# Attention backward on one core: dK, the dS transposes and dQ of a cell one step later, with their K load and dK store, and a fourth dS buffer

## The chip, the cores and the metric

One core of one Trainium2 chip. The metric is the device time of one execution in microseconds (us). All executions of the full kernels that are used here were classed as fast (not over 1.5% above the fastest execution of the same kernel beside them). Ratios are always the mean time of one kernel's fast runs over the mean of the other's fast runs of the same rounds, so they are not quite the ratio of the medians that stand beside them.

## The reference

Two independent attention blocks, A and B, forward and backward; all data are bf16. Cut to what matters:

```python
# per block: B, Sq, D = 8, 96, 640;  H, Sk, Dh = 32, 512, 128
q = (x @ wq).reshape(B, Sq, H, Dh).transpose(0, 2, 1, 3)
scores = jnp.einsum("bhqd,bhkd->bhqk", q, k_cache) * (Dh ** -0.5)
p = softmax(scores)
o = jnp.einsum("bhqk,bhkd->bhqd", p, v_cache)
out = o.transpose(0, 2, 1, 3).reshape(B, Sq, H * Dh) @ wo
# result: out of both blocks side by side, and the gradients of
# x, k_cache, v_cache, wq, wo of both blocks (jax.vjp)
```

## The kernel before

A *cell* is one head and one batch entry: 2 blocks x 32 heads x 8 entries = 512 cells. The kernel is a software pipeline. Every part of a cell is put into a list under a *step* number, the list is sorted by step and by a slot within the step, and is then emitted. A new cell starts in every step. Transfers serve two heads at once, a *pair* of cells, so each kind of transfer is issued once in two steps: its offset in `OFF` being even or odd decides which of the two.

```python
OFF = dict(kt=-1, vt=2, vn=1, kn=4, dv=7, dk=10, s2=3, s3=3, s4=4, s5=5, s6=6, s7=7, s8=8)
...
if j == 0:                                   # first cell of a pair
    em.add(ct + OFF["kt"], SLOTS["LOAD"], p_ldT(h, b, 0))         # K by DMA transpose
    em.add(ct + OFF["vt"], SLOTS["LOAD"], p_ldT(h, b, 1))         # V by DMA transpose
    em.add(ct + OFF["vn"], SLOTS["LOAD"] + 0.1, p_ldn(h, b, 1))   # V plain
    em.add(ct + OFF["kn"], SLOTS["LOAD"] + 0.1, p_ldn(h, b, 0))   # K plain
    em.add(ct + OFF["dv"], SLOTS["LOAD"] + 0.2, p_st(h, b, 1))    # store dV
    em.add(ct + OFF["dk"], SLOTS["LOAD"] + 0.2, p_st(h, b, 0))    # store dK
```

All six go through one queue, that of the sync engine, in the order of emission: `pools["sp"]` chains every transfer to the one before it. The transposed loads, the stores and their buffers:

```python
# p_ldT: 16 rows x (f d) of HBM -> [128, 64, 16], 4 buffers each for KT and VT
t_ = kvp.tile([128, F4 * KC, 16], BF16, name=key + "_p", bufs=4)
sp(nc.sync.dma_start_transpose(t_[:], src))
# p_st: dK and dV of a pair, 256 KB
sp(nc.sync.dma_start(dst.rearrange("h (p c) d -> p h (c d)", c=KC), t_[:]))
if which == 0:                               # after the dK store the cell's record is dropped
    for j in range(HP):
        CS.pop((blk, h + j, b))
...
st["dK_p"] = wk.tile([128, HP, KC * 128], BF16, name="dK_sb", bufs=3)   # three pairs of dK
```

The end of a cell. `c_s6` (offset s6) makes dP on TensorE and dS on VectorE. `c_s78` holds dQ of the cell at s8 and the transposes of dS of the cell at s7. `c_s7` (s7) makes dK from dS:

```python
# c_s6
nc.tensor.matmul(dP_ps[:], hs["dOT_h"][:, tok], st["VT"], start=True, stop=True)          # L386
dS_sb = wk.tile([Sq, Sk], BF16, name="dS_sb", bufs=3)
nc.vector.scalar_tensor_tensor(dS_sb..., dP_ps..., dl_ps[:, 0:1], st["P_sb"]..., ...)      # L390
# c_s78
nc.tensor.matmul(dQT_ps, st["K_sb"][:, c, :], st["dST_sb"]..., ...)                        # L405, dQ at s8
nc.tensor.transpose(dST_ps..., dS_sb[:, c * 128:(c + 1) * 128], ident[0:Sq, 0:Sq])         # L412, at s7
# c_s7
nc.tensor.matmul(dK_ps..., dS_sb..., hs["Qnat_h"]..., start=True, stop=True)               # L428
nc.scalar.activation(dK_p[:, j], dK_ps[:], ACT.Identity, scale=1.0)                        # L433
```

Projections, weight gradients and the output products of each head ("head work") are spread over the steps between these.

Of the kernel before, what the change touches and what calls it, by code (L numbers as in the profile page):

```python
# [11 lines left out]
BF16 = mybir.dt.bfloat16  # L12
# [28 lines left out]
SL_GRP = 95  # L41
SL_SETUP = 96

OFF = dict(kt=-1, vt=2, vn=1, kn=4, dv=7, dk=10, s2=3, s3=3, s4=4, s5=5, s6=6, s7=7, s8=8)
HP = 2
HK = [
    dict(pA=-10, pB=-7, pC0=[-6, -4], pC1=[-5, -3], pD1=-2, pD0=0, qA0=21, qA1=25, qB=[28, 25]),
# [24 lines left out]
def build_block(tc, em, tick0, blk, x, kc, vc, wq, wo, g_all, out_all, dx, dk, dv, dwq, dwo, ident, ones, pools, HG=4, first=True, groups=None):  # L72
    nc = tc.nc
    B, Sq, D = x.shape
    _, H, Sk, Dh = kc.shape
# [34 lines left out]
    const, ps, kvp, wk, hd, hst, grp = (pools[k] for k in ("const", "ps", "kvp", "wk", "hd", "hst", "grp"))  # L110

    def bank(shape, dt, name):
        return ps.tile(shape, dt, name=name, tag="bank")
# [75 lines left out]
    def pB(h):  # L189
        def f():  # L190
            st = HS[(blk, h)]
            woT_ps = bank([128, DC * 128], BF16, "woT_ps")
            for c in range(DC):
                nc.tensor.transpose(woT_ps[:, c * 128:(c + 1) * 128], st["wo_h"][:, c * 128:(c + 1) * 128], ident[:])
            woT_h = hd.tile([128, DC * 128], BF16, name="woT_h", bufs=1)
            evac(EV["pB0"], woT_h[:], woT_ps[:])
            st["woT_h"] = woT_h
            wqT_ps = bank([128, DC * 128], BF16, "wqT_ps")
            for c in range(DC):
                nc.tensor.transpose(wqT_ps[:, c * 128:(c + 1) * 128], st["wq_h"][:, c, :], ident[:])  # L200
            wqT_h = hst.tile([128, D], BF16, name="wqT_h")
            evac(EV["pB1"], wqT_h[:], wqT_ps[:])
            st["wqT_h"] = wqT_h
            st["QT_h"] = hd.tile([128, T], BF16, name="QT_h", bufs=4)
            st["dOT_h"] = hd.tile([128, T], BF16, name="dOT_h", bufs=4)
        return f
# [39 lines left out]
    def p_ldT(h, b, which):  # L246
        def f():
            key = "KT" if which == 0 else "VT"
            t_ = kvp.tile([128, F4 * KC, 16], BF16, name=key + "_p", bufs=4)
            src = (kc if which == 0 else vc)[b, h:h + HP].rearrange("h (r f) d -> (h r) (f d)", r=R8)  # L250
            sp(nc.sync.dma_start_transpose(t_[:], src))
            for j in range(HP):
                half = t_[:, :, j * R8:(j + 1) * R8]
                CS.setdefault((blk, h + j, b), {})[key] = half.rearrange("p (f c) r -> p f c r", c=KC)
        return f

    def p_ldn(h, b, which):
        def f():
            key = "K_sb" if which == 0 else "V_sb"
            t_ = kvp.tile([128, HP, KC, 128], BF16, name=key, bufs=4)  # L260
            src = (kc if which == 0 else vc)[b, h:h + HP]
            sp(nc.sync.dma_start(t_[:].rearrange("p h c d -> p h (c d)"), src.rearrange("h (p c) d -> p h (c d)", c=KC)))
            for j in range(HP):
                CS[(blk, h + j, b)][key] = t_[:, j]
        return f

    def p_st(h, b, which):
        def f():
            t_ = CS[(blk, h, b)]["dV_p" if which == 1 else "dK_p"]
            dst = (dv if which == 1 else dk)[b, h:h + HP]  # L270
            sp(nc.sync.dma_start(dst.rearrange("h (p c) d -> p h (c d)", c=KC), t_[:]))
            if which == 0:
                for j in range(HP):
                    CS.pop((blk, h + j, b))
        return f

    def h_alloc(h):
        def f():
            st = HS[(blk, h)]
            st["OT_h"] = hst.tile([128, T], BF16, name="OT_h", bufs=6)  # L280
            st["dQT_h"] = hst.tile([128, T], BF16, name="dQT_h")
        return f
# [97 lines left out]
    def c_s6(h, b):  # L380
        def f():
            st = CS[(blk, h, b)]
            hs = HS[(blk, h)]
            tok = slice(b * Sq, (b + 1) * Sq)
            dP_ps = bank([Sq, Sk], F32, "dP_ps")
            nc.tensor.matmul(dP_ps[:], hs["dOT_h"][:, tok], st["VT"], start=True, stop=True)  # L386
            dl_ps = bank([Sq, 1], F32, "dl_ps")
            nc.tensor.matmul(dl_ps[:], st["prod"][:], ones[:, 0:1], start=True, stop=True)  # L388
            dS_sb = wk.tile([Sq, Sk], BF16, name="dS_sb", bufs=3)
            nc.vector.scalar_tensor_tensor(dS_sb[:].rearrange("q (a f) -> q a f", f=F4), dP_ps[:].rearrange("q (f a) -> q a f", f=F4), dl_ps[:, 0:1],  # L390
                                           st["P_sb"][:].rearrange("q (a f) -> q a f", f=F4), op0=ALU.subtract, op1=ALU.mult)
            st["dS_sb"] = dS_sb
        return f
# [139 lines left out]
    for g in range(NG):  # L533
        h0 = GH0[g]
        for hh in range(groups[g]):
# [5 lines left out]
            em.add(c0t + hk["pB"], SL_HEAD, pB(h))  # L541
            em.add(c0t + OFF["s5"], SL_LOAD, h_alloc(h))
            for si in range(NTS):
# [4 lines left out]
            for b in range(B):  # L548
                ct = c0t + b * HP + j
                if j == 0:  # L550
                    em.add(ct + OFF["kt"], SLOTS["LOAD"], p_ldT(h, b, 0))
                    em.add(ct + OFF["vt"], SLOTS["LOAD"], p_ldT(h, b, 1))
                    em.add(ct + OFF["vn"], SLOTS["LOAD"] + 0.1, p_ldn(h, b, 1))
                    em.add(ct + OFF["kn"], SLOTS["LOAD"] + 0.1, p_ldn(h, b, 0))
                    em.add(ct + OFF["dv"], SLOTS["LOAD"] + 0.2, p_st(h, b, 1))
                    em.add(ct + OFF["dk"], SLOTS["LOAD"] + 0.2, p_st(h, b, 0))
# [156 lines left out]
```

## Time and profile before

| | kernel before |
|---|---|
| median of its first 3 timed runs | 1679.27 us (1679.18 to 1683.99) |
| span of the profiled run, a fourth (1674.12 us) | 1672.3 us, granted clock 0.994 |
| TensorE (PE) / VectorE (DVE) / ScalarE (ACT) / GpSimd (POOL) busy | 96 / 82 / 80 / 32% |
| dS transposes (L412) starting late, summed | 31.1 us |
| sum of all transfer issues of the one queue | 1460 us of 1672 |

The last row is worked out from the instruction records of the trace. A matmul starts late by its distance from the matmul before it, less the columns of that one divided by 2.4 per ns; gaps over 20 ns are summed. (The rate comes out of this trace: the median distance is 42 ns behind a matmul of 96 columns and 216 ns behind one of 512, so 416 columns more take 174 ns.)

From the page of the kernel before: part 1, the line of the sync engine's queue in part 3 (packets, MB, and the time of its packets as a share of the span of the 16 DMA engines), the first line of part 4 (the chain that ended last), and two groups of part 5, whose columns are busy time and mean ns of one, then idle time before it and what ended most of it.

```profile
PE 1607.8 (96%) x20640; PEld 1265.2 (76%) x20860; DVE 1366.7 (82%) x3381; ACT 1336.2 (80%) x3511; POOL 533.8 (32%) x1030
...
q1 hardware_dynamic: 378112, 454.57, 102.3%
...
PE 88%; DVE 5%; DMA 2%; issue 2%; ACT 2%; POOL 0%; SPq 0%; ACTq 0%; DVEq 0%
...
L433 ACT ACTIVATE dK_sb<-dK_ps 128x512 bf16<-128x512 f32 x512 | 303.2, 592 | 154.6 <-PE dK_ps L428 140.9
...
L412 PE MATMUL dq_dst_ps<-ident,dS_sb 96*128 96x96 bf16 x2048 | 173.2, 207 | 20.5 <-DVE dS_sb L390 20.3
```

By this chain TensorE is what bounds the kernel, and when it idles in mid-run, it is mostly before L412, for dS. From the waits of the kernel before (who waited for whom; us in total, times, longest):

```profile
ACT dK_sb L433 <- PE dK_ps L428: 140.9, 132, 2.7
...
PEld L412 <- DVE dS_sb L390: 27.0, 45, 1.5
...
PE dq_dst_ps L412 <- DVE dS_sb L390: 20.3, 43, 1.3
...
ACT dK_sb L433 <- DMA out_dram<-dK_sb: 10.4, 3, 4.9
```

One of these stalls in the timeline of the kernel before (start, duration in us, engine, line; in brackets the idle time and what ended it): dQ is done, and the transposes wait until dS, which began at 382.54, is there.

```profile
382.48 0.33 PE L405 MATMUL dq_dst_ps<-dST_sb,K_sb 128*128 128x96 bf16 x4
...
382.54 0.73 DVE L390 SCALAR_TENSOR_TENSOR dS_sb<-dP_ps,dl_ps,P_sb 96x512 bf16<-96x512 f32 x1
...
383.33 0.34 PE L412 MATMUL dq_dst_ps<-ident,dS_sb 96*128 96x96 bf16 x4 [0.52 <-DVE dS_sb L390]
```

The one DMA queue (SPq) of the kernel before in the timeline. These durations are the issue alone. The Trainium skill, "Perfetto Trace Analysis", section "Summary: the profiler window per engine type", says that the reported window of such a transfer hides the data movement, and the trace agrees: these issues take 0.4 to 1.7 us, while the median from issue to landing of a KT transpose is 5.1 us.

```profile
390.03 0.42 SPq L271 DMA_DIRECT2D out_dram<-dK_sb  x1
390.54 1.71 SPq L251 DMA_TRANSPOSE KT_p<-in_A_k_cache_dram  x1
392.35 0.53 SPq L262 DMA_DIRECT2D V_sb<-in_A_v_cache_dram  x1
392.97 0.42 SPq L271 DMA_DIRECT2D out_dram<-dV_sb  x1
393.48 1.17 SPq L251 DMA_TRANSPOSE VT_p<-in_A_v_cache_dram  x1
394.70 1.18 SPq L262 DMA_DIRECT2D K_sb<-in_A_k_cache_dram  x1
```

The two transposes of a pair, KT and VT, stand apart, with a load and a store between them on both sides.

### The profile page before, as it was taken

How to read it: one execution, taken by the hardware profiler on the slowest of the kernel's cores; microseconds unless marked ns; L12 is line 12 of the kernel's file. 1: busy time of each engine (PE TensorE's matmuls, PEld its weight loads, DVE VectorE, ACT ScalarE, POOL GpSimd, SP SyncE). 2: the span in 40 equal slices, each digit the busy share in tenths (PEclk: the TensorE clock that was granted, in tenths of full speed). 3: DMA queues.
4: the chain of work that ended last, by engine and by line, in shares of the span. 5: the costliest groups of instructions: out<-in, count | busy, mean ns of one | idle time of the engine just before them, and what ended most of it. 6: DMA issues, size and time to landing. Idle time of an engine off the chain costs nothing.

```text
span 1672.3 us, 55383 instructions
## 1 busy us (share of the span) xinstructions
PE 1607.8 (96%) x20640; PEld 1265.2 (76%) x20860; DVE 1366.7 (82%) x3381; ACT 1336.2 (80%) x3511; POOL 533.8 (32%) x1030
## 2 busy tenths in 40 slices
PE   6999999999999999999898999999999999999998
PEld 5777777777777787777676878777777777777776
DVE  4886888888888888888687778888888888888886
ACT  6988877879788787877776889788787877879783
POOL 2432333333233233333222333233333333333231
PEclk9999999999999999999899999999999999999999
DMA  9999999999999999999999999999999999999994
GB/s 247 283 266 285 266 268 296 297 270 275 271 279 281 285 268 292 265 284 233 275 290 297 295 266 272 278 287 274 274 291 281 278 286 281 283 274 273 282 271 139
DMA packets 378383, 458.13 MB, mean 274 GB/s; under 512 B 44288, under 2 KB 369920, under 8 KB 369920
## 3 DMA queue, kind: packets, MB, share of 16 engines
q1 hardware_dynamic: 378112, 454.57, 102.3%
q8 instruction: 163, 2.67, 0.7%
q14 instruction: 108, 0.88, 0.2%
HBM read 159.12 MB, written 159.12 MB: 190 GB/s over the span
## 4 chain that ended last, share of the span: by engine, by line
PE 88%; DVE 5%; DMA 2%; issue 2%; ACT 2%; POOL 0%; SPq 0%; ACTq 0%; DVEq 0%
PE q_ps L224 12%; PE o_ps L511 11%; PE dK_ps L428 6%; PE dV_ps L362 6%; PE dP_ps L386 6%; PE S_ps L291 6%; PE dwo_ps L466 6%; PE dwq_ps L486 6%; PE dq_dst_ps L412 5%; PE optp_ps L345 5%; PE optp_ps L338 5%; PE dq_dst_ps L405 4%; PE n_ps L239 4%; PE nat_ps L452 3%; DVE dS_sb L390 2%
## 5 line engine op out<-in xcount | busy, mean ns | idle before, releaser
L322 POOL TENSOR_SCALAR P_sb<-E_sb,rinv 96x512 bf16<-96x512 bf16 x512 | 352.5, 688 | 322.8 <-DVE rinv L313 321.6
L303 ACT ACTIVATE E_sb<-S_ps,negm 96x512 bf16<-96x512 f32 x512 | 348.2, 680 | 112.8 <-DVE negm L293 107.7
L376 POOL TENSOR_TENSOR prod<-OT_h,dOT_h 128x96 bf16<-128x96 bf16 x512 | 186.7, 365 | 784.6 <-DVE OT_h L348 768.1
L433 ACT ACTIVATE dK_sb<-dK_ps 128x512 bf16<-128x512 f32 x512 | 303.2, 592 | 154.6 <-PE dK_ps L428 140.9
L390 DVE SCALAR_TENSOR_TENSOR dS_sb<-dP_ps,dl_ps,P_sb 96x512 bf16<-96x512 f32 x512 | 383.2, 748 | 29.0 <-PE dl_ps L388 18.6
L293 DVE TENSOR_REDUCE negm<-S_ps 96x1 f32<-96x512 f32 x512 | 347.3, 678 | 60.7 <-PE S_ps L291 60.4
L367 ACT ACTIVATE dV_sb<-dV_ps 128x512 bf16<-128x512 f32 x512 | 308.1, 602 | 1.5 <-DMA out_dram<-dV_sb 1.3
L351 ACT ACTIVATE PT_sb<-optp_ps 128x384 bf16<-128x384 bf16 x512 | 251.7, 492 | 0.6 <-PE optp_ps L345 0.5
L414 DVE COPY dST_sb<-dq_dst_ps 128x384 bf16<-128x384 bf16 x512 | 177.6, 347 | 31.3 <-PE dq_dst_ps L412 28.8
L291 PE MATMUL S_ps<-KT_p,QT_h 128*96 128x512 bf16 x512 | 194.7, 380 | 5.7 <-ACT dK_sb L433 5.2
L428 PE MATMUL dK_ps<-Qnat_h,dS_sb 96*128 96x128 bf16 x2048 | 198.6, 220 | 0.4 <-ACT dK_sb L433 0.4
L362 PE MATMUL dV_ps<-dOnat_h,P_sb 96*128 96x128 bf16 x2048 | 198.7, 219 | 0.0
L386 PE MATMUL dP_ps<-VT_p,dOT_h 128*96 128x512 bf16 x512 | 195.7, 382 | 0.0
L412 PE MATMUL dq_dst_ps<-ident,dS_sb 96*128 96x96 bf16 x2048 | 173.2, 207 | 20.5 <-DVE dS_sb L390 20.3
L405 PEld LDWEIGHTS <-K_sb 128*128 128x128 bf16 x2048 | 133.9, 98 | 55.7 <-issue 9.5
L345 PE MATMUL optp_ps<-ident,P_sb 96*128 96x96 bf16 x2048 | 172.1, 205 | 2.2 <-POOL P_sb L322 1.5
L338 PE MATMUL optp_ps<-PT_sb,V_sb 128*128 128x96 bf16 x2048 | 172.6, 206 | 0.9 <-ACT PT_sb L351 0.8
L405 PE MATMUL dq_dst_ps<-dST_sb,K_sb 128*128 128x96 bf16 x2048 | 171.3, 206 | 0.0
L348 DVE CAST OT_h<-optp_ps 128x96 bf16<-128x96 f32 x512 | 127.0, 248 | 32.5 <-PE optp_ps L345 26.3
L511 PE MATMUL o_ps<-wo_r,OT_h 128*128 128x128 bf16 (+1 forms) x722 | 144.9, 295 | 2.5
L511 PE MATMUL o_ps<-wqT_h,dQT_h 128*128 128x128 bf16 (+1 forms) x721 | 144.4, 294 | 2.5
L224 PE MATMUL q_ps<-gT,woT_h 128*128 128x256 bf16 (+1 forms) x609 | 134.4, 324 | 9.7 <-DMA gT<-in_grad_out_dram 8.0
(66 smaller groups left out, 3012.8 us busy)
## 6 DMA issues: line engine op xcount, KB each, us to landing
out_dram<-dV_sb SPq DMA_DIRECT2D x256, 256.0 KB, 4.5
out_dram<-dK_sb SPq DMA_DIRECT2D x256, 256.0 KB, 4.5
V_sb<-in_A_v_cache_dram SPq DMA_DIRECT2D x128, 256.0 KB, 4.3
K_sb<-in_A_k_cache_dram SPq DMA_DIRECT2D x128, 256.0 KB, 4.4
V_sb<-in_B_v_cache_dram SPq DMA_DIRECT2D x128, 256.0 KB, 4.3
K_sb<-in_B_k_cache_dram SPq DMA_DIRECT2D x128, 256.0 KB, 4.3
out_dram<-dwo_sb SPq DMA_DIRECT2D x64, 160.0 KB, 4.6
out_dram<-dwq_sb SPq DMA_DIRECT2D x32, 320.0 KB, 4.5
```

Source lines behind the costliest of these rows:

```text
L224: nc.tensor.matmul(q_ps[:], lhs(c), rhsT[:, c, t0:t0 + w], start=(c == 0), stop=(c == DC - 1))
L293: nc.vector.tensor_reduce(negm[:], S_ps[:], axis=AX.X, op=ALU.max, negate=True)
L303: nc.scalar.activation(E_sb[:].rearrange("q (a f) -> q a f", f=F4), st["S_ps"][:].rearrange("q (f a) -> q a f", f=F4), ACT.Exp, bias=st["n ...
L322: nc.gpsimd.tensor_scalar(P_sb[:], st["E_sb"][:], st["rinv"][:], 0.0, op0=ALU.mult, op1=ALU.add)
L362: nc.tensor.matmul(dV_ps[:, c * 128:(c + 1) * 128], P_sb[:, c * 128:(c + 1) * 128], hs["dOnat_h"][:, b * 128:(b + 1) * 128], start=True, s ...
L367: nc.scalar.activation(dV_p[:, j], dV_ps[:], ACT.Identity, scale=1.0)
L386: nc.tensor.matmul(dP_ps[:], hs["dOT_h"][:, tok], st["VT"], start=True, stop=True)
L390: nc.vector.scalar_tensor_tensor(dS_sb[:].rearrange("q (a f) -> q a f", f=F4), dP_ps[:].rearrange("q (f a) -> q a f", f=F4), dl_ps[:, 0:1] ...
L405: nc.tensor.matmul(dQT_ps, st["K_sb"][:, c, :], st["dST_sb"][:, c * Sq:(c + 1) * Sq], start=(c == 0), stop=(c == KC - 1))
L428: nc.tensor.matmul(dK_ps[:, c * 128:(c + 1) * 128], dS_sb[:, c * 128:(c + 1) * 128], hs["Qnat_h"][:, b * 128:(b + 1) * 128], start=True, s ...
L433: nc.scalar.activation(dK_p[:, j], dK_ps[:], ACT.Identity, scale=1.0)
L511: nc.tensor.matmul(o_ps[:], src[:, t * 128:(t + 1) * 128], rhs, start=(hh == 0), stop=(hh == groups[g] - 1))
```

## The change

The intent: the dS transposes should not wait for a dS that was only just made. dK, the dS transposes and dQ of a cell move one step later (s7, s8), dS lives one step longer and gets a fourth buffer. The K load, which feeds dQ, and the dK store follow by one step; the dK store has to, because it drops the cell's record.

```diff
-OFF = dict(kt=-1, vt=2, vn=1, kn=4, dv=7, dk=10, s2=3, s3=3, s4=4, s5=5, s6=6, s7=7, s8=8)
+OFF = dict(kt=-1, vt=2, vn=1, kn=5, dv=7, dk=11, s2=3, s3=3, s4=4, s5=5, s6=6, s7=8, s8=9)
...
-            dS_sb = wk.tile([Sq, Sk], BF16, name="dS_sb", bufs=3)
+            dS_sb = wk.tile([Sq, Sk], BF16, name="dS_sb", bufs=4)
```

## The prediction

> **What bounds the kernel now.** TensorE. The page shows PE busy 96% of 1672.3 us, DVE 82%, ACT 80%, POOL 32%; the chain of waits is 88% PE, 5% DVE, 2% each DMA, ACT and issue. Busy share overstates PE (the Trainium skill, "Perfetto Trace Analysis", section "Identifying the Most-Contended Engine"), so I used start-to-start times. In full stretches four 96-column matmuls take 0.17 us, 43 ns each, which agrees with columns / 2.4 GHz + about 2.5 ns ("TensorE: Matmul & The Clock Gate", "Wait — 56ns, not 53.3ns?"). Over the whole trace the streamed columns come to 1465 us and the small per-matmul excess to 56 us; the remaining 139 us are gaps before matmuls that started over 20 ns late. Those before the dS transposes (line 412) are 31.1 us: 7.3 in the first 130 us, 7.6 from 130 to 785, 2.7 to 1000, 8.2 to 1615, 5.2 in the tail. The list of waits agrees: PE weight loads of line 412 waited 27.0 us for DVE dS (45 times), the matmuls 20.3 (43 times). In the steady state it recurs twice per four heads (100.8 us): a visible 0.52 us where a cell step has no head work, and 0.25 us.
>
> **What the change does.** It adds and removes no work. A step's PE order stays dQ, dS transposes, dK, O, P transposes, dV, dP, S, but the dS it uses was made two steps ago (a step is 2.2 to 4.5 us) instead of just before, behind dP (0.38), the wait for the row sum and DVE's 0.75 us. So that wait should vanish. The fourth dS buffer keeps DVE from waiting for dK. K load and dK store move with their users, so distances in steps (4 from load to use, 2 from dK to store) stay; the transfers bunch in odd steps, but the in-order queue runs ahead of them anyway. The dx groups follow one step later as well: the last of them (4 matmuls, about 0.33 us) then falls in the very step that had no head work and showed the 0.52 us stall.
>
> **How much is on the critical path.** At most about 31 us. Not all returns: in those light steps ACT's own work is near the step's length (in the tail 0.33 us idle of 2.59 us), and its P^T copy or POOL's P becomes the next thing PE waits for. Estimate by region: tail about 8 steps x 0.3 = 2.5 us; start 4 of 7; steady 11 of 18. Sum 17 us; minus 1 to 2 us for one more step at the drain. Hiccups around 120, 797 and 915 us (ACT waiting for dK_sb's store, 10.4 us in 3 waits; the second block's gT) stay, give or take 4 us.
>
> **Predicted:** 1665 us, 8 times in 10 between 1655 and 1677. Faster by over 2%: 0.04; within 2%: 0.94; slower by over 2%: 0.02.
>
> **Signs that each step is right.** PE's wait of line 412 for dS falls from 20.3 us to under 3, the weight loads' from 27.0 to under 4. ACT's wait for dK_ps (140.9 us, 132 times) falls by 10 to 30. New PE waits at lines 338 (ACT PT_sb) and 345 (POOL P_sb), 3 to 10 us together. Tail steps shorten from 2.58 to about 2.3 us. Busy times per engine and ns per instruction unchanged within 1%. Nothing of the DMA becomes a large new wait.
>
> **What would make it wrong.** If light steps are bound by ACT or DVE throughput, the wait only changes its name and the gain is under 5 us. If bunched transfers make dK_sb's or K's landing later, ACT or line 405 waits for a DMA and the change may be lost. If many small late starts elsewhere (line 224 32.6 us, 511 21.5 us) are echoes of dS, the gain exceeds 25 us.

## More of the kernel before

The two lines of the instructions on tile KT_p, kernel before (one per block; shortest, median and longest issue in ns):

```profile
L251 SPq DMA_TRANSPOSE KT_p<-in_A_k_cache_dram x128: 1102/1197/3641, 4.3 to 807.4; - x128
L251 SPq DMA_TRANSPOSE KT_p<-in_B_k_cache_dram x128: 1106/1187/2971, 814.0 to 1619.3; - x128
```

## The result, and the profile after

The changed kernel took 1739.99 us (median of 4 runs, 1735.23 to 1752.61) beside 1681.63 us for the kernel before: ratio 1.0354, 95% interval 1.0288 to 1.0419. It is slower by 3.5%, and outside the predicted range.

From the page of the changed kernel, the same lines:

```profile
PE 1626.3 (94%) x20670; PEld 1274.0 (73%) x20860; DVE 1367.1 (79%) x3381; ACT 1333.8 (77%) x3511; POOL 533.4 (31%) x1030
...
PE 67%; DMA 12%; ACT 9%; DVE 6%; issue 5%; SPq 0%; POOL 0%; ACTq 0%; DVEq 0%; POOLq 0%
...
L433 ACT ACTIVATE dK_sb<-dK_ps 128x512 bf16<-128x512 f32 x512 | 304.7, 595 | 248.8 <-PE dK_ps L428 152.8
...
L412 PE MATMUL dq_dst_ps<-ident,dS_sb 96*128 96x96 bf16 x2048 | 173.7, 207 | 0.0
```

The idle time before L412 has gone from 20.5 us to 0.0, as intended; its late starts fell from 31.1 to 1.4 us. But DMA now has 12% of the chain where it had 2%. The waits of the changed kernel:

```profile
ACT dK_sb L433 <- PE dK_ps L428: 152.8, 121, 2.7
ACT dK_sb L433 <- DMA out_dram<-dK_sb: 91.3, 53, 6.3
...
PE dwo_ps L466 <- ACT dK_sb L433: 29.8, 15, 3.1
...
PE woT_ps L194 <- ACT dK_sb L433: 14.8, 9, 4.5
```

ScalarE may not overwrite a dK buffer before the store of three pairs ago has landed. It waited 91.3 us for that (before: 10.4), and the evictions behind it (copies of TensorE's results out of PSUM, its output memory) waited too. TensorE then waited for ScalarE ("PE ... <- ACT dK_sb"). Lines 466 and 194 do not read dK; in this code all their results share one pool of PSUM banks with dK, so a bank is what they must have waited for. One such wait in the timeline of ScalarE, changed kernel:

```profile
424.79 0.62 ACT L367 ACTIVATE dV_sb<-dV_ps 128x512 bf16<-128x512 f32 x1
428.55 0.60 ACT L433 ACTIVATE dK_sb<-dK_ps 128x512 bf16<-128x512 f32 x1 [3.14 <-DMA out_dram<-dK_sb]
429.04 0.67 ACT L303 ACTIVATE E_sb<-S_ps,negm 96x512 bf16<-96x512 f32 x1
```

Why had the store not landed? Its data had been ready long before. From the trace, the median time from the end of a pair's last dK eviction to the issue of its store went from 4.9 us to 10.5 us; the store itself took no longer (median issue to landing 4.5 and 4.0 us). So the stores stood in the queue. The queue of the changed kernel in the timeline:

```profile
399.38 2.36 SPq L251 DMA_TRANSPOSE VT_p<-in_A_v_cache_dram  x1
401.83 1.54 SPq L251 DMA_TRANSPOSE KT_p<-in_A_k_cache_dram  x1
403.46 0.53 SPq L262 DMA_DIRECT2D K_sb<-in_A_k_cache_dram  x1
404.09 0.42 SPq L262 DMA_DIRECT2D V_sb<-in_A_v_cache_dram  x1
404.60 0.43 SPq L271 DMA_DIRECT2D out_dram<-dK_sb  x1
405.12 1.47 SPq L271 DMA_DIRECT2D out_dram<-dV_sb  x1
406.68 1.10 SPq L251 DMA_TRANSPOSE VT_p<-in_A_v_cache_dram  x1
407.88 1.81 SPq L251 DMA_TRANSPOSE KT_p<-in_A_k_cache_dram  x1
```

With kn = 5 and dk = 11, all transfers but VT fall into the odd steps. KT is the first in the odd step and VT the only one in the even step, so the two transposes of the queue are now neighbours. The two lines of tile KT_p in the changed kernel:

```profile
L251 SPq DMA_TRANSPOSE KT_p<-in_A_k_cache_dram x128: 1102/1749/4535, 3.9 to 842.8; - x128
L251 SPq DMA_TRANSPOSE KT_p<-in_B_k_cache_dram x128: 1101/1788/3797, 849.3 to 1686.8; - x128
```

The median issue of a KT transpose grew from 1.19 us to 1.76 us. Where KT comes straight after VT (183 times) the mean is 1.99 us; before, where it came straight after the dK store (184 times), it was 1.42 us. These longer issues are not waits for a free KT buffer: in the changed kernel the last matmul that read the buffer (L291) had ended 12.7 us (median) before the KT issue began, and less than 0.3 us before it in one of 252 pairs only.

Where the time went. Sixteen steps at a time, between the starts of every sixteenth dP matmul, the kernel before alternates between 55.4 us (much head work) and 45.4 us (little). In the changed kernel the medians are 54.1 and 51.6 us. The heavy half gained 1.3 us, the light half lost 6.2.

### The profile page after: what moved, and what is told of

It is laid out like the page before. It is cut to its first block, busy times and chain, and to the rows that moved or that the text cites. A ratio compares the mean times of both kernels' runs of the same rounds, so it can differ in the third digit from the quotient of the medians.

```text
span 1734.5 us, 55579 instructions
## 1 busy us (share of the span) xinstructions
PE 1626.3 (94%) x20670; PEld 1274.0 (73%) x20860; DVE 1367.1 (79%) x3381; ACT 1333.8 (77%) x3511; POOL 533.4 (31%) x1030
## 3 DMA queue, kind: packets, MB, share of 16 engines
q1 hardware_dynamic: 378112, 454.57, 97.1%
## 4 chain that ended last, share of the span: by engine, by line
PE 67%; DMA 12%; ACT 9%; DVE 6%; issue 5%; SPq 0%; POOL 0%; ACTq 0%; DVEq 0%; POOLq 0%
PE o_ps L511 10%; PE q_ps L224 9%; DMA out_dram<-dK_sb 9%; PE dwo_ps L466 5%; PE dwq_ps L486 5%; PE S_ps L291 4%; PE dV_ps L362 4%; PE dP_ps L386 4%; PE dK_ps L428 4%; PE optp_ps L338 4%; PE optp_ps L345 3%; PE dq_dst_ps L405 3%; PE dq_dst_ps L412 3%; PE n_ps L239 3%; ACT E_sb L303 3%
## 5 line engine op out<-in xcount | busy, mean ns | idle before, releaser
L433 ACT ACTIVATE dK_sb<-dK_ps 128x512 bf16<-128x512 f32 x512 | 304.7, 595 | 248.8 <-PE dK_ps L428 152.8
L291 PE MATMUL S_ps<-KT_p,QT_h 128*96 128x512 bf16 x512 | 195.8, 382 | 5.1 <-ACT E_sb L303 2.2
L412 PE MATMUL dq_dst_ps<-ident,dS_sb 96*128 96x96 bf16 x2048 | 173.7, 207 | 0.0
L466 PE MATMUL dwo_ps<-g_nat,Onat 128*128 128x128 bf16 (+1 forms) x736 | 133.6, 303 | 32.6 <-ACT dK_sb L433 29.8
L313 DVE RECIPROCAL rinv<-rowsum 96x1 f32<-96x1 f32 x512 | 79.3, 155 | 104.5 <-ACT E_sb L303 90.5
```

The lines of the kernel that those rows point to most:

```text
L291: nc.tensor.matmul(S_ps[:], hs["QT_h"][:, tok], st["KT"], start=True, stop=True)
```

## The experiments

**The theory**: two DMA transposes that are neighbours in the queue take more of its time than two that are spaced. The queue had little to spare, and now falls behind, until the three dK buffers run out. **Rival 1**: the later dK, dS transposes and dQ cost something themselves (buffers, PSUM banks). **Rival 2**: five transfers in one step are too bunched, or the dK stores come too late in steps. **Rival 3**: four reads in a row and then two writes are bad for the transfers. All full kernels gave correct results; those of transfers alone gave wrong ones on purpose.

The first four were compared on one chip, on which the kernel before took 1695.04 us (median of 7, 1684.51 to 1708.21).

### split_back: the compute part of the change, with the old places of K load and dK store

```diff
 (against the changed kernel)
-OFF = dict(... kn=5, dv=7, dk=11, ... s7=8, s8=9)
+OFF = dict(... kn=4, dv=7, dk=10, ... s7=8, s8=9)
+ (the dropping of the cell's record is moved out of the dK store, two steps later)
```

> The change with its compute part whole (dS transposes, dK and dQ one step later, fourth dS buffer) but K load and dK store back in the even steps, so that the queue alternates again: KT transpose, V, dV store, VT transpose, K, dK store. Theory (the order in the one DMA queue is what costs: VT and KT transposes now stand next to each other, and the queue needs about 6.2 us for a pair of cells where it needed 5.7): about 1662 us, ratio to before 0.985 to 0.995, ACT's wait of dK_sb for its store under 15 us, no line-412 wait. Rival 1 (the later dS/dK/dQ itself costs): near 1735 us, ratio 1.03. Rival 2 (dK stores come too late in steps): also fast here, as the store comes one step after dK instead of two.

Measured: 1677.45 us, ratio 0.99 (0.9828 to 0.9971). The 91.3 us of dK waits for stores are 7.4 us, and L412 waits for dS no more. But ScalarE now waits 25.7 us in 30 waits for dV stores (before: 1.3), which I had not expected, and the time is not the 1662 us expected, although the ratio is as it was. Rival 1 falls: the compute part alone does not slow the kernel. The alternating queue is still close to its limit.

### kt_middle: everything in the steps of the change, only the order within the odd step differs

```diff
 (against the changed kernel)
-em.add(ct + OFF["kt"], SLOTS["LOAD"], p_ldT(h, b, 0))
+em.add(ct + OFF["kt"], SLOTS["LOAD"] + 0.15, p_ldT(h, b, 0))
```

> The change whole, all transfers in the same steps as in it; only within the odd step the KT transpose is issued after the K and V loads, so the queue reads VT, K, V, KT, dK store, dV store. Theory (adjacent transposes): fast, about 1662 us, ratio 0.985 to 1.0; issue of a KT transpose falls from a mean of about 1.9 us to 1.4 us; dK_sb waits for its store under 20 us. Rival 2 (five transfers bunched in one step, or stores queued behind loads): stays near 1735 us, ratio 1.03, as the steps are unchanged. Rival 3 (four reads in a row, then two writes): stays slow too.

Measured: 1653.97 us, ratio 0.9762 (0.9703 to 0.982). This one slot number puts KT behind the K and V loads, and the kernel is 86 us faster than the changed kernel was (1739.99 to 1653.97 us, of different submissions; against the kernel before the ratio went from 1.0354 to 0.9762). Rivals 2 and 3 fall: the bunching, the steps, and the sequence of four reads and two writes are the same as in the changed kernel. The queue in the timeline of kt_middle; between the transposes stand two loads on one side and two stores on the other:

```profile
393.45 1.15 SPq L251 DMA_TRANSPOSE KT_p<-in_A_k_cache_dram  x1
394.69 0.53 SPq L271 DMA_DIRECT2D out_dram<-dK_sb  x1
395.31 0.42 SPq L271 DMA_DIRECT2D out_dram<-dV_sb  x1
395.82 1.18 SPq L251 DMA_TRANSPOSE VT_p<-in_A_v_cache_dram  x1
397.10 0.55 SPq L262 DMA_DIRECT2D K_sb<-in_A_k_cache_dram  x1
397.74 0.42 SPq L262 DMA_DIRECT2D V_sb<-in_A_v_cache_dram  x1
398.21 1.10 SPq L251 DMA_TRANSPOSE KT_p<-in_A_k_cache_dram  x1
```

One line of its waits, and its two lines of tile KT_p:

```profile
ACT dK_sb L433 <- DMA out_dram<-dK_sb: 6.4, 3, 4.9
```

```profile
L251 SPq DMA_TRANSPOSE KT_p<-in_A_k_cache_dram x128: 1101/1111/4147, 4.5 to 799.0; - x128
L251 SPq DMA_TRANSPOSE KT_p<-in_B_k_cache_dram x128: 1101/1106/5088, 804.9 to 1602.2; - x128
```

The median issue of KT is 1.11 us (the mean fell to 1.30 us, lower than the 1.4 expected), dK's waits for its stores come to 6.4 us, and the dK store is issued 3.3 us (median) after its data are ready, instead of 10.5.

### dma_only: the kernel before, with only K load and dK store moved

```diff
 (against the kernel before)
-OFF = dict(... kn=4, dv=7, dk=10, ... s7=7, s8=8)
+OFF = dict(... kn=5, dv=7, dk=11, ... s7=7, s8=8)
```

> The kernel before with only K load and dK store one step later (dS, dK, dQ and the three dS buffers as before). Theory: the queue has the changed order, VT next to KT, so it is slow, 1730 to 1760 us, ratio 1.03 to 1.05, with dK_sb waits of 80 us or more and the line-412 waits still there (20 us or so). Rival 1 (the later compute costs): near before, ratio within 1%.

Measured: 1749.09 us, ratio 1.0333 (1.0269 to 1.0397), with 99.9 us of dK waits for stores and 20.6 us of L412 waits for dS still there. The whole loss comes with the two moved transfers, without any of the compute:

```profile
ACT dK_sb L433 <- DMA out_dram<-dK_sb: 99.9, 49, 4.4
...
PE dq_dst_ps L412 <- DVE dS_sb L390: 20.6, 43, 1.6
```

One thing besides the order differs here: dK itself did not move, so its store comes one step later after it than in the two kernels. mid_only below has the same distance and is fast, so the distance is not the cause.

### adj_before: the kernel before, with only the KT transpose one step earlier, beside VT

```diff
 (against the kernel before)
-OFF = dict(kt=-1, ...)
+OFF = dict(kt=-2, ...)
```

> The kernel before with only the KT transpose issued one step earlier, in the even steps beside VT: the queue reads VT, KT, K, dK store, V, dV store. Nothing of compute, no store and no other load moves, and reads and writes alternate as much as before apart from the pair. Theory (adjacent transposes): slow, ratio 1.02 to 1.05, the KT issue mean rises from 1.4 to about 1.9 us, dK_sb and dV_sb waits for stores grow from 11 to 60 us or more. Rivals 1, 2 and 3: no change beyond 1%.

Measured: 1846.69 us, ratio 1.0897 (1.0826 to 1.0967). The direction is as expected, and the size twice what I expected. KT's mean issue is 2.40 us (expected 1.9), and the dK waits for stores are 175.1 us. No store and no other load moved, and reads and writes alternate, so the neighbourhood of the transposes is enough to make the loss, in the kernel before as well.

### deep_stores: the changed kernel with more store buffers

```diff
 (against the changed kernel)
-dV_p ... name="dV_sb", bufs=3     +dV_p ... name="dV_sb", bufs=4
-dK_p ... name="dK_sb", bufs=3     +dK_p ... name="dK_sb", bufs=4
-dS_sb ... bufs=4                  +dS_sb ... bufs=3
```

> The change as it is, adjacent transposes and all, with four instead of three buffers for dK and for dV pairs (three for dS, to fit in memory). Theory (the queue's throughput is short in the light stretches and three buffers run out): one more pair of slack, about 6 us, takes away most but not all of the waits for stores: 91 us falls to 10 to 50 us, time 1685 to 1715 us, ratio 1.0 to 1.02; the KT transposes stay slow (mean about 1.9 us behind VT). Rival (buffers too few by design, queue fast enough): as fast as the best variant, 1655 us.

Measured: 1736.95 us beside 1682.27 us for the kernel before on that chip, ratio 1.031 (1.027 to 1.0349). My expectation missed: the buffers gave nothing. (That dS has three buffers here costs nothing in the fast variant, see mid_ds3; it was not tried alone in this order.) No large dK wait for a store is left, but TensorE waits for loads instead. Lines of its waits:

```profile
PEld L386 <- DMA VT_p<-in_B_v_cache_dram: 10.7, 6, 5.5
...
PEld L194 <- DMA wo_r<-in_A_wo_dram: 10.2, 6, 2.3
...
PEld L405 <- DMA K_sb<-in_B_k_cache_dram: 7.5, 11, 1.8
```

So the queue is not late for a while and then catches up: with neighbouring transposes it is the bound of nearly the whole run. The trace of the changed kernel agrees: the gaps of over 0.15 us between the queue's issues sum to 37 us of 1734 (before: 66 of 1672).

The sums agree. I took from the traces the time from one dK store's issue to the next where just one pair's six transfers lie between and both stores had been ready for over 1 us, so that the queue was backed up: median 5.75 us before (114 cases), 6.17 us in the changed kernel (123). The transfers of weights and their gradients, with the gap behind each, add 7.6 and 8.1 us per 16 pairs. As an estimate from these, 16 pairs need 16 x 5.75 + 7.6 = 100 us of queue before and 16 x 6.17 + 8.1 = 107 us after; the measured 32 steps took 55.4 + 45.4 = 100.8 and 54.1 + 51.6 = 105.7 us. The queue already was nearly as long as TensorE's work, and became longer.

### mid_only: the kernel before, with K load, dK store and KT as in kt_middle

```diff
 (against the kernel before)
-OFF = dict(... kn=4, dv=7, dk=10, ... s7=7, s8=8)
+OFF = dict(... kn=5, dv=7, dk=11, ... s7=7, s8=8)
-em.add(ct + OFF["kt"], SLOTS["LOAD"], p_ldT(h, b, 0))
+em.add(ct + OFF["kt"], SLOTS["LOAD"] + 0.15, p_ldT(h, b, 0))
```

> The kernel before with K load and dK store one step later and the KT transpose between the loads and the stores, so the queue has the order VT, K, V, KT, dK store, dV store; dS, dK and dQ stay where they were. It splits the gain of the fast variant (ratio 0.976). Theory: the later dS is worth 15 to 20 us as predicted, so this kernel keeps the line-412 waits (about 20 us on PE) and is 0.985 to 1.0 of before. Rival: the queue order alone makes the gain: ratio 0.976 here too.

Measured: 1670.09 us, ratio 0.9923 (0.9894 to 0.9952), with the L412 wait of 20.4 us still there. So the new queue order alone is worth about 0.8% in the timed runs, and the rest of kt_middle's gain comes with the later dS. Where the 0.8% lies the traces do not show: the profiled runs of the two kernels differ by 1.1 us only (1671.2 and 1672.3), and 32 steps take 55.4 + 45.4 us in both.

### kt_middle_2: the fast variant again, in the rounds of mid_only

> The fast variant again, on this chip, to compare with the two above: ratio 0.97 to 0.985.

Measured: 1653.22 us, ratio 0.9825 (0.9787 to 0.9863). Against mid_only in the same rounds, the later dS, dK and dQ with the fourth buffer save 1670.09 - 1653.22 = 16.9 us. kt_middle is the best of all versions that I ran, and it beats both kernels; whether by more or less than 2% the runs leave open.

### mid_ds3: kt_middle with three dS buffers

```diff
 (against kt_middle)
-dS_sb = wk.tile([Sq, Sk], BF16, name="dS_sb", bufs=4)
+dS_sb = wk.tile([Sq, Sk], BF16, name="dS_sb", bufs=3)
```

> The fast variant (change whole, KT transpose between loads and stores) with three dS buffers instead of four. If the fourth buffer carries part of the gain, this is slower by 5 us or more and DVE dS shows waits for PE dK; my expectation is the same time, ratio 0.97 to 0.985, since the dK that frees the buffer is a whole step earlier than the dS that needs it.

Measured: 1652.97 us, ratio 0.9816 (0.9788 to 0.9845), the same as with four. The fourth dS buffer of the change buys nothing.

### The queue by itself

Seven kernels with no arithmetic: 256 pairs of the same transfers through the same queue, from and to the same shapes. Each ran once: q_mid, q_alt, q_adj and q_adjalt on one chip, q_gap1, q_tr and q_cp on another. The pair time is the distance between the first and the last issue of one kind, divided by 255; the weight transfers are left out.

```diff
 (the kernels differ in this line; q_tr has the stores added at its end)
 q_mid     ORDER = ["VT", "K", "V", "KT", "dK", "dV"]      # kt_middle
 q_gap1    ORDER = ["VT", "K", "KT", "V", "dK", "dV"]
 q_alt     ORDER = ["KT", "V", "dV", "VT", "K", "dK"]      # the kernel before
 q_adj     ORDER = ["VT", "KT", "K", "V", "dK", "dV"]      # the changed kernel
 q_adjalt  ORDER = ["VT", "KT", "K", "dK", "V", "dV"]      # adj_before
 q_tr      ORDER = ["VT", "KT"]                            # stores follow after all of them
 q_cp      ORDER = ["K", "V", "dK", "dV"]
```

> Transfers alone, no arithmetic (wrong results on purpose: zeros are stored): 256 pairs of the same six transfers through the same one queue, in the order of the kernel before: KT, V, dV store, VT, K, dK store. Theory (adjacent transposes): this is the shorter of the two, about 4.8 to 5.3 us a pair (the fastest backed-up pairs before took 4.8). Rivals: the same pair time in all four orders, within 3%.

> The same transfers alone in the order of the changed kernel: VT, KT, K, V, dK store, dV store. Theory: 0.4 us or more per pair longer than the alternating order (5.4 us or more), so over 100 us longer in all. Rivals: same within 3%.

> The same transfers alone in the order VT, K, V, KT, dK store, dV store. Theory: within 3% of the alternating order. If four reads and then two writes were what costs, it is as slow as the changed order.

> The same transfers alone in the order VT, KT, K, dK store, V, dV store: the transposes adjacent, loads and stores alternating. Theory: as slow as the changed order or slower. If grouping of reads and writes were the cost, it is as fast as the alternating order.

> Only the 512 transposes, VT and KT in turn, through the one queue (wrong results on purpose; the stores follow after all of them, so that the outputs exist). If a transpose has to wait for room that the one before it still takes, a pair of transposes alone takes about as long as it does adjacent in the mixed orders, VT 1.5 plus KT 1.9 us, 3.4 us or more. If a transpose in itself is cheap and only copies in front of it slow it, 2.3 to 2.5 us (the shortest issues seen were 1.1 us each).

> Only the four plain transfers of a pair (wrong results on purpose). Their issues took 0.47 to 0.58 us, so 2.1 to 2.3 us a pair if the issue is the limit[...]. With the run of transposes alone it shows whether transposes and copies overlap: if the two sums exceed the 5.23 us of the best mixed order, mixing hides part of a transpose behind copies, and adjacency gives that up.

> All six transfers, VT, K, KT, V, dK store, dV store: one copy between the two transposes on one side, three on the other. If spacing is what counts, between the best order (5.23 us a pair, two and two) and the adjacent one (5.64): 5.3 to 5.55. If only strict adjacency costs, 5.2 to 5.3.

| run | pair, us | mean issue VT, us | mean issue KT, us | the full kernel with this order, us |
|---|---|---|---|---|
| q_mid | 5.23 | 1.73 | 1.12 | 1653 to 1654 (dS later), 1670 (not) |
| q_gap1 | 5.33 | 1.58 | 1.37 | not run |
| q_alt | 5.35 | 1.41 | 1.56 | 1677 (dS later), 1678 to 1708 (not) |
| q_adj | 5.64 | 1.50 | 1.88 | 1740 (dS later), 1749 (not) |
| q_adjalt | 6.15 | 1.16 | 2.65 | 1847 (not) |
| q_tr | 2.64 | 1.29 | 1.25 | |
| q_cp | 2.74 | | | |

In q_alt the pair is a little over the 4.8 to 5.3 us expected. q_adj is 0.28 us longer, less than the 0.4 expected; q_mid is within 3% of q_alt, as expected. Without any compute the orders come out in the same rank as the full kernels, and nearly all that differs is the issue of the transposes: VT and KT together take 2.85 us in q_mid, 3.37 in q_adj and 3.81 in q_adjalt, the four copies 2.10, 1.98 and 2.06. Neighbourhood is not the whole story, though. In q_adj and in q_adjalt the transposes are neighbours alike, and yet alternating the loads and stores behind them costs 0.51 us more; why, no run here shows. Here are the KT lines of q_mid and q_adj, from the instructions of their transposing line:

```profile
L55 SPq DMA_TRANSPOSE KT_p<-in_A_k_cache_dram x128: 1108/1109/1518, 72.6 to 735.8; - x128
```

```profile
L55 SPq DMA_TRANSPOSE KT_p<-in_A_k_cache_dram x128: 1207/1844/2368, 71.5 to 788.1; - x128
```

The last three runs were made to find out why. Transposes alone are cheap: 2.64 us for two neighbours, well below the 3.4 us expected if each had to wait for room that the one before it takes. So that reason, taken alone, falls. The parts alone sum to 2.64 + 2.74 = 5.38 us: the best mixed order is a little below that, at 5.23, and the neighbouring ones are above, at 5.64 and 6.15. Two neighbouring transposes are thus expensive only among copies. One copy between them on one side and three on the other, q_gap1, is at 5.33, at the edge of the two ranges expected. q_alt, with two copies on both sides, is no faster at 5.35, so these runs do not show that spacing counts by degrees: most of the loss is gone with that one copy. (The copies alone came out at 2.74 us. In their trace the four issues take 1.59 us of that, so the issue alone is not their limit; what holds the queue in the gaps of 0.30 us, median, between them, the trace does not name.) The DMA engines are not fuller in the slow orders: the queue's packets took 103.4% of the 16 engines' span in q_mid, 95.5% in q_adj and 93.4% in q_adjalt. What inside the queue or the DMA engines makes this so, the traces do not show, and it stays open.

## Why the prediction was wrong

- **Right: the wait of L412 for dS.** Predicted to fall from 20.3 us to under 3; there is none left (idle before L412: 0.0 us).
- **Right in size, once the queue is mended, but in part by luck: the worth of the later dS.** Predicted 17 us from the regions of the trace, less 1 to 2 at the end; kt_middle_2 against mid_only measured 16.9 us, with runs of one kernel up to 7.6 us apart. The traces of the two do not put all of it where I looked for it. Of 32 steps, the light 16 held 0.83 us of the late starts of L412 and the heavy 16 held 0.41; but the light ones became slower (45.4 to 45.8 us) and the heavy ones faster by more than their stall (55.4 to 54.1). The sum, 0.9 us per 32 steps, fits; the split does not, and its cause stays open.
- **Right: new waits of TensorE at lines 338 and 345.** Predicted 3 to 10 us; in the changed kernel 4.7 us for PT_sb and 3.2 us for P_sb (before: 0.8 and 1.5), in kt_middle_2 3.9 and 3.7.
- **Partly right: the tail.** The last 15 steps took 38.2 us before and 36.3 us in kt_middle_2, 2.55 and 2.42 us each; predicted was 2.3.
- **Wrong: ScalarE's wait for dK_ps** was to fall by 10 to 30 us; it rose, from 140.9 to 152.8 us (168.5 in kt_middle_2). So this wait was not an echo of the dS stalls.
- **Wrong, and the step that failed:** "the transfers bunch in odd steps, but the in-order queue runs ahead of them anyway", and with it "Nothing of the DMA becomes a large new wait". The queue did not run ahead. In the kernel before, the median dK store was already issued 4.9 us after its data were ready, and the issues filled 1460 of 1672 us, with gaps of over 0.15 us between them of 66 us in all. I counted distances in steps, which the change keeps, and took the bunching to be a matter of timing, where it was a matter of order: it made KT the neighbour of VT. That costs 0.42 us per pair in the backed-up queue (5.75 to 6.17 us), and made the queue, no longer TensorE, the bound.
- **Missing in the risks:** "If bunched transfers make dK_sb's or K's landing later ... the change may be lost" named the right symptom, but I gave a slowdown of over 2% a chance of 0.02.

The Trainium skill, "Perfetto Trace Analysis", section "What "DMA-bound" means", lists the issuing engine's sequencer being solid with DMA slices as one of the ways to be DMA-bound. By that sign this kernel was near its limit before the change: from 100 to 700 us the trace shows TensorE busy 98% of the time and the same queue issuing one transfer after the other, its issues filling 89% and most of the rest being gaps of under 0.1 us. By the estimate above (100 us of queue in 100.8 us) the two limits were about one per cent apart. The page's chain shows only the first. A hint of the second stood on the page, which the prediction passes over: the queue's packets took 102.3% of the 16 engines' span. But that reading does not tell the kernels apart in the right direction: it is 101.4% in kt_middle, 97.1% in the changed kernel and 92.2% in adj_before.

## What to carry to other kernels

Before moving a transfer by a step, write down the order in which the queue will issue all transfers and how much of the span their issues fill; distances in steps say nothing of either. Where one queue carries DMA transposes among plain copies and has little to spare, try to keep the transposes apart: here one slot number, 0.15, took the ratio from 1.035 to 0.976. Here more store buffers did not help a queue that was the bound on average (1737 us with four, 1740 with three), and a fourth dS buffer did not help either (1653 us with three and with four). And where a predicted sum comes true, look in the trace whether its parts did.

## What the Trainium skill lacked or had wrong

- "DMA: Bandwidth & Descriptors" (sections "DMA Transpose (X-bar)" and "Rules for kernel authors") says nothing of what the order of transposes and copies within one queue costs. Here the same six transfers took 5.23 us a pair with the transposes spaced, and 5.64 or 6.15 us with them as neighbours; the full kernel went from 1653 to 1740 us by that order.
- The same page, section "Latency and other measured facts", gives an effective bandwidth of 261 GB/s for DMA transposes with a non-contiguous middle dimension and about 350 to 400 GB/s for contiguous ones. The run of transposes alone (16 rows of 16 KB each) moved 199 GB/s from 100 to 700 us; the copies alone moved 382 GB/s. In the run of transposes the issues filled 96% of the queue's time, so it may be the issue that held it, and the page's figure is not refuted for larger transfers.
- No page gives the time that the issue of a DMA transpose of 256 KB takes on trn2 ("DMA: Bandwidth & Descriptors" has sequencer cycles for small tiles only). Here it was 1.10 us at the least, against 0.37 us at the least for a copy of the same 256 KB.
- "TensorE: Matmul & The Clock Gate" (section "Wait — 56ns, not 53.3ns?") held: it gives N / 2.4 GHz + about 2.5 ns from start to start, 42.5 ns for 96 columns, and here the median was 42 ns.
